# Gated linear attention and routed experts on one core: first rows stored later, banks returned later, a second alpha first, and early products of a second layer

## The chip, the core and the metric

The kernel runs on one core of a Trainium2 chip. The metric is the device time of one execution in microseconds (us). Five engines are named below: PE (TensorE, the matrix engine, with its weight loads PEld), DVE (VectorE), ACT (ScalarE), POOL (GpSimd) and SP (SyncE, which issues nearly all DMAs). Each engine works through its own instructions in the order in which the kernel emits them. PSUM has eight banks, which the kernel hands out as tiles.

## What is computed

The first half is a recurrent attention over 4 batches of 8 heads, 768 positions each, head size 48:

```python
for t in range(S):
    state = alpha[:, :, t, :, None] * state + einsum('bhd,bhde', k[:, :, t], v[:, :, t])
    y[:, :, t] = einsum('bhd,bhde->bhe', q[:, :, t], state)
```

The second half takes the 3072 rows of 384 numbers that come out and sends each to the one of eight experts with the largest logit of `x @ w_gate`. The expert computes `relu(x @ w1[e]) @ w2[e]` with 1024 hidden numbers, and the result is scaled by the softmax weight of that expert. Everything is float32.

## The kernel before

The 3072 rows are 24 chunks of 128 positions. A chunk `s` needs four loads (`load`, L300 to L309), one each of alpha, k, q and v. They are called a, k, q, v with the chunk's number below: a10 is alpha of chunk 10. Per chunk the kernel does this:

- `logs` (L328, ACT): logarithm of alpha. `cums` (L338): one PE product with a triangular mask gives cumulative sums in the single PSUM tile `cum`, from which ACT takes two exponentials, `icp` (L344) and `cpb` (L345). The next chunk's product can go into `cum` when `cpb` has been read out.
- `operands` (L360, mostly POOL): k times `icp` and q times `cpb`. `transposes` (L368): PE turns both, ACT and DVE copy them out as `kT` and `qT`.
- `scores` (L380), `reads`, `weighs`, `products`, `state`: the attention of the chunk and the state for the next. `rows` (L473) and `keep_rows` (L481) make the chunk's 128 output rows in the tile `xs`; `store_rows` (L489, SP) writes them to the DRAM tensor `x_rows`.

The order is written out by hand, under a manual schedule. Lines 631 to 700 start chunks 0 to 6. The loop of line 702 takes two chunks `s`, `s+1` in a pass, s = 2, 4, ..., 20. In a pass the calls for several chunks are mixed: `logs` and `cums` for s+5 and s+6, `operands` likewise, `transposes` for s+3 and s+4, `scores` for s+2 and s+3. SP's queue in a pass holds nine loads (`more_loads(2)`, `(2)`, `(5)` from the list `to_load`, L316), two small decay transfers and two stores of rows. Loads wait for nothing but a free buffer: a, k and q have five each, v has six; `xs` has three.

`keep_busy(n)` (L613) issues n products of a zero tile, whose result nobody reads. In the trace one float32 product is two matmul instructions.

After the loop the last two chunks are finished and the routing is worked out: `choose`, `slots_of`, `one_hots` on DVE, rank products and `tokens_of_slots` on PE (L589) into the tile `route`, then `slots(0)` (L605, DVE), which reads `route`, and the gathers of rows by POOL (L271). Each gathered block of 128 rows is turned by PE (`turn`, L966) and copied out by DVE into `xT`. The rows of expert 0's first 256 slots (`EB` = 2 blocks) are known earlier, so their first layer is emitted by a generator, `first_layer` (L787); `go_ahead(n)` takes its next n products, which serve as work for PE between the steps of the routing. It has 24 products (8 blocks `f` of the hidden layer by 3).

PSUM changes hands in this stretch: the pool `ps` (tiles `tp` with two banks, `sA`, `sB`, `xr`, `y0`, `y1`) is closed at L852, and `mps` (`hp` with three banks, `xtp` and `zp` with two each) takes the same seven banks.

The rest, from about 155 us on, is the eight experts in turn: `layer1` (L974), `layer2` (L987) and a scatter of finished rows by POOL (L1000), with the weights fetched ahead by SP.

Of the kernel before, what the change touches and what calls it, by code (L numbers as in the profile page):

```python
# [8 lines left out]
F32 = mybir.dt.float32  # L9
# [9 lines left out]
def kernel(  # L19
# [31 lines left out]
    C = 128  # L51
# [237 lines left out]
    with tc.tile_pool(name="ld", bufs=6) as ld, \  # L289
# [21 lines left out]
        def some_loads(names):  # L311
# [2 lines left out]


        to_load = [  # L316
            (n, x + d) for x in range(7, NT + 2)
            for n, d in (
                (("a", 1), ("k", 0), ("q", 0), ("v", -2)) if x == 7 else (("k", 0), ("v", -2), ("a", 1), ("q", 0))
            )  # L320
        ]


        def more_loads(n):
            for _ in range(min(n, len(to_load))):
# [42 lines left out]
        def transposes(s):  # L368
            d = st[s]
            for i, n in enumerate(("kT", "qT")):  # L370
                tp = ps.tile([C, NP, C], F32, name="tp", bufs=2)
                for p in range(NP):
                    nc.tensor.transpose(tp[:, p, :], pair(kqb[s % 4][:, i], p), ident[:])  # L373
                d[n] = work.tile([C, NP, C], F32, name=n, bufs=2 + i)
                if i:
                    nc.vector.tensor_copy(d[n][:], tp[:])  # L376
                else:
                    nc.scalar.copy(d[n][:], tp[:])
# [102 lines left out]

        def keep_rows(s):
            d = st[s]
            xs = work.tile([C, W], F32, name="xs", bufs=3)
            nc.scalar.copy(xs[:, :Dm].rearrange("t (p c) -> t p c", p=NP), d["xr"][:, :, :D2])  # L485
            nc.gpsimd.tensor_copy(xs[:, Dm:], lgn[:, s, :])
            d["xs"] = xs

        def store_rows(s):  # L489
            r0 = s * C + (s >= NT // 2)  # L490
            nc.sync.dma_start(x_d[r0 : r0 + C, :], st[s]["xs"][:])

        def choose(g):

# [133 lines left out]
        nc.scalar.preload_act_table_set("natural_log_exp_and_others")  # L628
        hots = []

        some_loads("a0 k0 q0 a1 k1 q1")
        first_consts()
        keep_busy(5)
        back_consts()
        for i in range(4):
            late_consts(i)
        logs(0)
        cums(0)
        keep_busy(3)
        operands(0, nc.vector, nc.vector)  # L640
        some_loads("a2 v0")
        decay_out(0, nc.scalar)
        logs(1)
        transposes(0)
        cums(1)
        operands(1)
        decay_in(0, nc.scalar)
        scores(0)
        keep_busy(3)
        some_loads("v1 k2 q2 a3 v2")  # L650
        logs(2)
        transposes(1)
# [48 lines left out]
        parts = fetch_parts(0)  # L701
        for s in range(2, NT - 2, 2):
            more_loads(2)
            if s == 2:
                store_rows(0)
            do(decay_out, s + 4)
            more_loads(2)

            for _ in range(8 if s > NT - 8 else 0):
                next(parts, None)  # L710
            y = results_of(s)
            reads(s)
            reads(s + 1)

            weighs(s, 0)
            weighs(s, 1)
            products(s + 1)
            products(s + 2)
            weighs(s + 1, 0)
            results_to(s, y, 0)  # L720
            weighs(s + 1, 1)
            results_to(s, y, 1)
            state(s + 1)
            do(logs, s + 5)
            if hots:
                one_hots(hots.pop(0))
            scores(s + 2)
            do(logs, s + 6)
            do(cums, s + 5)
            ranks = y[0][:].rearrange("r i p t -> r (i p t)")  # L730
            ranked = [rank_products(g, ranks[:, : len(g) * E]) for g in groups_of if g[-1] == s - 1]
            counts = ranks[:, C : C + E]
            if s in (TE, ORD):

                nc.tensor.matmul(
                    counts, lhsT=ones_sq[:], rhs=ohs[:, s, :], start=True, stop=True, skip_group_check=True,
                )
            if s == ORD:
                early_slots(ranks[:, 2 * C : 2 * C + EB * NQ])
                fetch_lot(0)  # L740
            for r in ranked if s < ORD else ():
                slots_of(*r)
            transposes(s + 3)
            do(operands, s + 5)
            state(s + 2)
            rows(s)
            keep_rows(s)
            store_rows(s - 1)
            if s == ORD:
                for r in ranked:  # L750
                    slots_of(*r)
                key = standing(counts[0:1, :])
                one_hots(hots.pop(0))
                one_hots(hots.pop(0))
                route = rps.tile([C, Dm], F32, name="cum")
                tokens_of_slots(0, TE)
            do(cums, s + 6)
            do(transposes, s + 4)
            more_loads(5)
            do(decay_in, s + 4)  # L760
            rows(s + 1)
            keep_rows(s + 1)
            if s == TE:
                close_early(counts[0:1, 0:1])

            chosen = [g for g in groups_of[:-2] if g[-1] == s + 1] + ([groups_of[-2]] if s == ORD else [])
            for g in chosen:
                choose(g)
            if hots and not chosen:
                one_hots(hots.pop(0))  # L770
            scores(s + 3)
            do(operands, s + 6)
            for g in chosen:
                sums(g)
            store_rows(s)
            if s == 2:

                nc.sync.dma_start(x_d[N // 2 : N // 2 + 1, :], zero_w[:])
            late_consts(s + 2)
            late_consts(s + 3)  # L780
            if hots and chosen:
                one_hots(hots.pop(0))
            for _ in range(4 if s == NT - 8 else 0):
                next(parts, None)
        for _ in parts:
            pass
        def first_layer():  # L787
            for f in range(FB):
                if f < 2:
                    hp = ps.tile([C, NP, C], F32, name="tp", bufs=2)[:].rearrange("r p t -> r (p t)")  # L790
                else:
                    hp = mps.tile([C, CAP], F32, name="hp", bufs=3)
                for a in range(DB):
                    nc.tensor.matmul(  # L794
                        hp[:, :EC], lhsT=w_t[0][0][:, a, f * C : (f + 1) * C], rhs=xT[0][:, a, :EC],
                        start=(a == 0), stop=(a == DB - 1),
                    )
                    if a < DB - 1:
                        yield
                nc.scalar.activation(h_t[0][:, f, :EC], hp[:, :EC], AF.Relu)  # L800
                yield

        ahead = first_layer()

        def go_ahead(n):
# [7 lines left out]
        y = results_of(s)  # L813
        reads(s)
        reads(s + 1)
        store_rows(s - 1)
        weighs(s, 0)
        weighs(s, 1)
        weighs(s + 1, 0)
# [8 lines left out]
            nc.scalar.copy(xT[0][:, :, k * C : (k + 1) * C], tp[:, :DB, :])  # L828
        rows(s)
        keep_rows(s)  # L830
        store_rows(s)
        go_ahead(3)
        for _ in range(3):
            one_hots(hots.pop(0))
        turns(key)
        rows(s + 1)
        keep_rows(s + 1)
        store_rows(s + 1)
        choose(groups_of[-1])
        sums(groups_of[-1])  # L840
        tokens_of_slots(TE, NT - 4)
# [3 lines left out]
        for i, (p, c, r) in enumerate((  # L845
# [3 lines left out]
        )):  # L849
            nc.tensor.matmul(p, lhsT=c[:], rhs=r, start=(i == 0), stop=(i == 2), skip_group_check=True)  # L850
        slots_of(groups_of[-1], pos)
        banks.close()  # L852
        mps = ctx.enter_context(tc.tile_pool(name="moe_ps", bufs=2, space=PSUM))
        go_ahead(4)
        one_hots(hots.pop(0))
        one_hots(hots.pop(0))
        tokens_of_slots(NT - 4, NT)
        nc.tensor.matmul(
            route[:, NC : NC + E], lhsT=ones_sq[:], rhs=ohs[:, NT, :], start=False, stop=True, skip_group_check=True,
        )  # L860
# [126 lines left out]
    def layer2(parts, gw, idx, apart):  # L987

        zp = mps.tile([C, Dm], F32, name="zp")
        wd = C if len(parts) == 1 else min(m for *_, m in parts)  # L990
        cuts = [(w2, h, c) for w2, h, c0, m in parts for c in range(c0, c0 + m, wd)]
        for f in range(FB):
            for i, (w2, h, c) in enumerate(cuts):
                nc.tensor.matmul(  # L994
                    zp[i * wd : (i + 1) * wd, :], lhsT=h[:, f, c : c + wd], rhs=w2[:, f, :],
                    start=(f == 0), stop=(f == FB - 1), skip_group_check=True,
                )
        zo = wk.tile([C, Dm], F32, name="zo", bufs=3)
        nc.scalar.activation(zo[:], zp[:], AF.Copy, scale=gw)  # L999
        ins = nc.gpsimd.indirect_dma_start(  # L1000
            out=out[:, :], out_offset=bass.IndirectOffsetOnAxis(ap=idx, axis=0),
            in_=zo[:], in_offset=None, bounds_check=N - 1, oob_is_err=False,
        )
        if apart:
            ins = getattr(ins, "ins", ins)
            tc.declare_no_dep(ins, group="rows_out", reason="disjoint rows")
            tc.add_to_no_dep_group("rows_out", ins)
# [20 lines left out]
        turn(*rows_t[k], *to)  # L1028

    def results(k):  # L1030
        parts = []
        for i in range(E):
            a, b = within(i, k)
# [14 lines left out]

    for i in range(E):
        if i == 0:  # L1050
            go_ahead(10)
            for k in range(EB, needed[0][-1] + 1):
                turn_block(k)
                go_ahead(3)
            go_ahead(99)
            layer1(w_t[0][0], xT[0], h_t[0], EC, cols[0])
        else:
            if i == E - 1:
# [84 lines left out]
```

## Time and profile before

| | us |
|---|---|
| median of three runs | 428.0 (427.19, 428.0, 1521.73) |
| the profiled execution, its own time | 427.69 |
| its span in the profile | 425.9 |
| PE busy | 418.0 |
| POOL / DVE / ACT busy | 141.0 / 138.3 / 108.0 |

The span is from the first to the last instruction of the profile; the time of the execution holds 1.8 us more around it. In the page's table of 40 slices each digit is the busy share, in tenths, of a stretch of about 10.6 us. The attention loop covers roughly 29 to 137 us, the routing 137 to 155 us, and the experts the rest.

### The profile page before, as it was taken

To read this page: it belongs to the slowest core of one execution; us is meant where nothing else is said; L and a number is where in the kernel's file an instruction comes from. 1 tells how busy PE (TensorE), PEld (TensorE's weight loads), DVE (VectorE), ACT (ScalarE), POOL (GpSimd) and SP (SyncE) were. 2 spreads that over 40 slices of the span, in tenths; PEclk is the share of its full clock that TensorE was granted. 3 is DMA by queue.
4 is the path that set the end of the run, shared out by engine and by line. 5 is a ranking of instruction groups with operands and counts; after the bars stand their busy time and mean duration, and the time that the engine had idled before them with its cause. 6 is when DMAs were issued, how large, how long until landed. Compare 5 with 4: busy or idle time off the path is not lost.

```text
span 425.9 us, 7698 instructions
## 1 busy us (share of the span) xinstructions
PE 418.0 (98%) x2990; PEld 283.5 (67%) x2990; DVE 138.3 (32%) x414; ACT 108.0 (25%) x230; POOL 141.0 (33%) x256
## 2 busy tenths in 40 slices
PE   8999999999999999999999999999999999999995
PEld 6888788888889887555554556655655455555452
DVE  6434567575768734712011101101201201111100
ACT  4565555555542221111111111011111110011011
POOL 5396677576675150250160120034010010011011
PEclk9999999999999999999999999999999999999999
DMA  8999998999976144994543600814720050000000
GB/s 172 181 174 209 187 204 186 204 206 212 186 212 208 56 115 143 393 372 152 179 133 94 234 32 0 304 45 112 246 94 12 5 181 20 0 33 20 1 33 30
DMA packets 132576, 59.43 MB, mean 140 GB/s; under 512 B 114614, under 2 KB 127452, under 8 KB 132538
## 3 DMA queue, kind: packets, MB, share of 16 engines
q1 hardware_dynamic: 127720, 48.96, 44.7%
q0 software_dynamic: 3328, 9.94, 7.1%
q8 instruction: 24, 0.39, 0.4%
q10 hardware_dynamic: 1490, 0.02, 0.2%
q14 instruction: 14, 0.11, 0.1%
HBM read 49.32 MB, written 9.98 MB: 139 GB/s over the span
## 4 chain that ended last, share of the span: by engine, by line
PE 61%; issue 28%; POOL 5%; SPq 2%; DMA 2%; ACT 1%; POOLq 0%; DVE 0%; ACTq 0%
PE zp L994 16%; PE hp L978 14%; PE sA L386 5%; PE y L430 5%; PE xr L478 4%; PE tp L373 4%; PE cum L341 3%; POOL out_dram L1000 3%; PE y L418 2%; PE hp L794 2%; PE xr L618 2%; PE xtp L970 1%; POOL xg L271 1%; PE sB L452 1%; DMA a_sb<-in_alpha_dram 1%
## 5 line engine op out<-in xcount | busy, mean ns | idle before, releaser
L994 PE MATMUL zp<-w,h_sb 128*128 128x384 f32 (+2 forms) x560 | 137.1, 487 | 0.0
L978 PE MATMUL hp<-xT,w 128*128 128x416 f32 (+5 forms) x384 | 123.9, 483 | 0.1
L994 PEld LDWEIGHTS zp<-w,h_sb 128*128 128x128 f32 (+2 forms) x560 | 73.6, 163 | 56.4 <-issue 14.8
L978 PEld LDWEIGHTS hp<-xT,w 128*128 128x128 f32 x384 | 71.6, 190 | 51.1 <-issue 31.0
L1000 POOL DMA_INDIRECT out_dram<-zo,o_idx x26 | 25.8, 991 | 213.5 <-ACT zo L999 208.5
L983 DVE TENSOR_SCALAR h_sb<-hp 128x416 f32<-128x416 f32 (+5 forms) x32 | 17.7, 554 | 148.1 <-PE hp L978 140.9
L999 ACT ACTIVATE zo<-zp,gw 128x384 f32<-128x384 f32 x26 | 15.1, 581 | 123.7 <-PE zp L994 114.5
L985 ACT ACTIVATE h_sb<-hp 128x416 f32<-128x416 f32 (+5 forms) x32 | 15.6, 487 | 106.5 <-PE hp L978 99.1
L271 POOL DMA_INDIRECT xg<-x_rows,g_idx x26 | 25.1, 966 | 11.1 <-issue 6.7
L386 PE MATMUL sA<-qT,kT 48*128 48x128 f32 x192 | 27.7, 284 | 0.2 <-DVE qT L376 0.2
L386 PE MATMUL sB<-qT,kT 48*128 48x128 f32 x192 | 27.7, 285 | 0.0
L972 DVE COPY xT<-xtp 128x384 f32<-128x384 f32 (+3 forms) x29 | 13.1, 485 | 44.6 <-PE xtp L970 43.2
L386 PEld LDWEIGHTS sA<-qT,kT 48*128 48x128 f32 x192 | 23.1, 187 | 4.7 <-issue 2.3
L364 POOL TENSOR_TENSOR kqb<-k_sb,icp 128x384 f32<-128x384 f32 x23 | 23.1, 1005 | 8.9 <-ACT icp L344 8.7
L430 PE MATMUL y<-dA,vb 128*64 128x128 f32 x192 | 25.9, 277 | 0.0
L373 PE MATMUL tp<-ident,kqb 128*128 128x128 f32 x192 | 25.4, 274 | 0.2 <-POOL kqb L366 0.2
L430 PE MATMUL y<-dB,vb 128*64 128x128 f32 x192 | 25.4, 277 | 0.0
L373 PEld LDWEIGHTS tp<-ident,kqb 128*128 128x128 f32 x192 | 21.8, 141 | 5.4 <-issue 2.7
L478 PE MATMUL xr<-back,yT 128*128 128x104 f32 x192 | 25.1, 274 | 0.0
L478 PEld LDWEIGHTS xr<-back,yT 128*128 128x128 f32 x192 | 23.6, 192 | 0.8 <-ACT xs L485 0.2
L376 DVE COPY qT<-tp 128x512 f32<-128x512 f32 x24 | 16.6, 690 | 21.0 <-PE tp L373 20.9
L386 PEld LDWEIGHTS sB<-qT,kT 48*128 48x128 f32 x192 | 23.1, 187 | 0.0
(179 smaller groups left out, 433.9 us busy)
## 6 DMA issues: line engine op xcount, KB each, us to landing
w<-in_moe_w_dram SPq DMA_DIRECT2D x14, 1536.0 KB
x_rows<-xs SPq DMA_DIRECT2D x24, 196.0 KB
a_sb<-in_alpha_dram SPq DMA_DIRECT2D x24, 192.0 KB
k_sb<-in_k_dram SPq DMA_DIRECT2D x24, 192.0 KB
q_sb<-in_q_dram SPq DMA_DIRECT2D x24, 192.0 KB
vb<-in_v_dram SPq DMA_DIRECT2D x24, 192.0 KB
w<-in_moe_w_dram SPq DMA_DIRECT2D x12, 128.0 KB
w<-in_moe_w_dram SPq DMA_DIRECT2D x8, 192.0 KB
```

What stands on the lines that cost most here:

```text
L271: nc.gpsimd.indirect_dma_start(out=xg[:, j, :], out_offset=None, in_=x_d[: N + 1 if n else TE * C + 1, :], in_offset=bass.IndirectOffsetOn ...
L364: k.tensor_tensor(kq[:, 0, :, :D], d["k"][:], heads(d["icp"]), op=ALU.mult)
L373: nc.tensor.transpose(tp[:, p, :], pair(kqb[s % 4][:, i], p), ident[:])
L376: nc.vector.tensor_copy(d[n][:], tp[:])
L386: nc.tensor.matmul(t[:, p, :], lhsT=d["kT"][r : r + D, p, :], rhs=d["qT"][r : r + D, p, :], start=True, stop=True,)
L430: nc.tensor.matmul(d["y"][h][at(p, a) : at(p, a) + DP, n, :], lhsT=d["v"][:, 2 * p + a, :], rhs=d["d" + "AB"[a]][:, p, :], start=(first an ...
L478: nc.tensor.matmul(xr[:, p, :], lhsT=d["yT"][:, p // (NP // 2), p % (NP // 2), :], rhs=back[:, p, :], start=True, stop=True)
L978: nc.tensor.matmul(hp[:, c0:c1], lhsT=w1[:, a, f * C : (f + 1) * C], rhs=xT[:, a, c0:c1], start=(a == 0), stop=(a == DB - 1),)
L983: nc.vector.tensor_relu(h[:, f, c0:c1], hp[:, c0:c1])
L985: nc.scalar.activation(h[:, f, c0:c1], hp[:, c0:c1], AF.Relu)
L994: nc.tensor.matmul(zp[i * wd : (i + 1) * wd, :], lhsT=h[:, f, c : c + wd], rhs=w2[:, f, :], start=(f == 0), stop=(f == FB - 1), skip_group ...
L1000: ins = nc.gpsimd.indirect_dma_start(out=out[:, :], out_offset=bass.IndirectOffsetOnAxis(ap=idx, axis=0), in_=zo[:], in_offset=None, bound ...
```

## The change

- `to_load` keeps its order, but for one place: alpha of chunk 10 is now loaded before v of chunk 7.
- The start loads a1 directly behind a0; it has one idle product fewer before chunk 0's cumulative sums (4 for 5), takes `logs(1)` straight behind `logs(0)`, puts `cums(1)` ahead of `transposes(0)`, and leaves out the three idle products after `scores(0)`. For chunk 0 alone, DVE copies `kT` and ACT copies `qT`; for the others it stays the other way.
- Rows are stored by a counter. The pass s=2 stores none (before: rows 0, 1 and 2), s=4 stores 0 and 1 (before: 3 and 4), s=6 stores 2, 3, 4 (before: 5 and 6), s=8 stores 5 to 8 (before: 7 and 8); from s=10 it is as before. `xs` has six buffers.
- `first_layer` uses `tp` for its first four blocks `f` instead of two, and goes on, after its 24 products, with the second layer of the two early blocks (16 products of 384 columns, into `zp`). `ps` is closed after `tokens_of_slots` and two more products of the generator. There are 12 products before the closing and 9 after it (before: 6 before and 14 after), then a turn, 3 products, a turn and 3 products again. The scaling and scatter of `layer2` become the function `write`, which `results` calls for the early blocks.

```diff
         to_load = [
-            (n, x + d) for x in range(7, NT + 2)
-            for n, d in (
-                (("a", 1), ("k", 0), ("q", 0), ("v", -2)) if x == 7 else (("k", 0), ("v", -2), ("a", 1), ("q", 0))
-            )
+            (n, x + {"a": 1, "v": -2}.get(n, 0)) for x in range(7, NT + 2)
+            for n in {7: "akqv", 9: "kavq"}.get(x, "kvaq")
         ]
...
-                if i:
+                if i == (s > 0):
                     nc.vector.tensor_copy(d[n][:], tp[:])
...
-            xs = work.tile([C, W], F32, name="xs", bufs=3)
+            xs = work.tile([C, W], F32, name="xs", bufs=6)
...
+        to_store = list(range(NT))
+
+        def stores(n):
+            for _ in range(n):
+                store_rows(to_store.pop(0))
...
-        some_loads("a0 k0 q0 a1 k1 q1")
+        some_loads("a0 a1 k0 q0 k1 q1")
         first_consts()
-        keep_busy(5)
+        keep_busy(4)
...
         logs(0)
+        logs(1)
         cums(0)
         keep_busy(3)
         operands(0, nc.vector, nc.vector)
         some_loads("a2 v0")
         decay_out(0, nc.scalar)
-        logs(1)
+        cums(1)
         transposes(0)
-        cums(1)
         operands(1)
         decay_in(0, nc.scalar)
         scores(0)
-        keep_busy(3)
...
-            if s == 2:
-                store_rows(0)
             do(decay_out, s + 4)
...
-            store_rows(s - 1)
+            stores({2: 0, 8: 2}.get(s, 1))
...
-            store_rows(s)
+            stores({2: 0, 6: 2, 8: 2}.get(s, 1))
...
         def first_layer():
             for f in range(FB):
-                if f < 2:
+                if f < 4:
...
+            for k in range(EB):
+                zps[k] = mps.tile([C, Dm], F32, name="zp")
+                for f in range(FB):
+                    nc.tensor.matmul(
+                        zps[k][:], lhsT=h_t[0][:, f, k * C : (k + 1) * C], rhs=w_t[0][1][:, f, :],
+                        start=(f == 0), stop=(f == FB - 1), skip_group_check=True,
+                    )
+                    if f == FB - 1:
+                        zdone.add(k)
+                    yield
...
         slots_of(groups_of[-1], pos)
-        banks.close()
-        mps = ctx.enter_context(tc.tile_pool(name="moe_ps", bufs=2, space=PSUM))
         go_ahead(4)
         one_hots(hots.pop(0))
         one_hots(hots.pop(0))
         tokens_of_slots(NT - 4, NT)
+        go_ahead(2)
+        banks.close()
+        mps = ctx.enter_context(tc.tile_pool(name="moe_ps", bufs=2, space=PSUM))
...
     def results(k):
+        if k < EB:
+            while k not in zdone:
+                next(ahead)
+            write(zps[k], gw[k], o_idx[:, k : k + 1], True)
+            return
...
-            go_ahead(10)
+            go_ahead(9)
             for k in range(EB, needed[0][-1] + 1):
                 turn_block(k)
                 go_ahead(3)
-            go_ahead(99)
```

More of the change, by code (lines that the diff above doesn't have):

```diff
@@ L801, in first_layer @@
                 yield
+            for k in range(EB):
[8 more added lines that the diff above has]
+                    yield
+        zps, zdone = {}, set()
         ahead = first_layer()
@@ L815 @@
         reads(s + 1)
-        store_rows(s - 1)
+        stores(1)
         weighs(s, 0)
@@ L830 @@
         keep_rows(s)
-        store_rows(s)
+        stores(1)
         go_ahead(3)
@@ L837 @@
         keep_rows(s + 1)
-        store_rows(s + 1)
+        stores(1)
         choose(groups_of[-1])
@@ L997, in layer2, with write @@
                 )
+        write(zp, gw, idx, apart)
+    def write(zp, gw, idx, apart):
         zo = wk.tile([C, Dm], F32, name="zo", bufs=3)
```

## The prediction

> **What bounds the kernel now.** I read the page first: the engines' busy time, then the slices.
>
> ```profile
> PE 418.0 (98%) x2990; PEld 283.5 (67%) x2990; DVE 138.3 (32%) x414; ACT 108.0 (25%) x230; POOL 141.0 (33%) x256
> ...
> PEclk9999999999999999999999999999999999999999
> DMA  8999998999976144994543600814720050000000
> ```
>
> PE is busy for 418.0 of 425.9 us at the full granted clock, so PE's own queue is the path, and only what PE waits for, or what it does in vain, can be saved. The DMA row says something else beside it: in the first ten slices, 0 to about 106 us, the 16 DMA engines are as full as PE. Next, the waits of PE:
>
> ```profile
> PE xr L618 <- DVE still L118: 1.3, 1, 1.3
> PE cum L341 <- ACT cpb L345: 0.6, 1, 0.6
> PE hp L794 <- ACT h_sb L800: 0.4, 1, 0.4
> ```
>
> Beyond the first, which is the launch, they come to little more than 1 us. The change touches the second and the third. Then PE's timeline of the start (start, duration, engine, line):
>
> ```profile
> 1.25 3.82 PE L618 MATMUL xr<-still 128*128 128x256 f32 x10 [1.25 <-DVE still L118]
> 5.00 0.88 PE L341 MATMUL cum<-ln,cmask 128*128 128x384 f32 x2
> 5.72 1.46 PE L618 MATMUL xr<-still 128*128 128x256 f32 x6
> 7.14 1.06 PE L373 MATMUL tp<-ident,kqb 128*128 128x128 f32 x8
> 8.05 0.81 PE L341 MATMUL cum<-ln,cmask 128*128 128x384 f32 x2
> ...
> 10.18 1.56 PE L618 MATMUL xr<-still 128*128 128x256 f32 x6
> 11.57 1.04 PE L373 MATMUL tp<-ident,kqb 128*128 128x128 f32 x8
> ```
>
> Busy is not useful here: L618 are idle products, and the six at 10.18 hold 1.39 us, start to next start. Third, the wait inside the loop, in ACT's and PE's timelines:
>
> ```profile
> 46.21 0.52 ACT L330 ACTIVATE ln<-a_sb 128x384 f32<-128x384 f32 x1 [1.29 <-DMA a_sb<-in_alpha_dram]
> ```
>
> ```profile
> 45.90 1.04 PE L478 MATMUL xr<-back,yT 128*128 128x104 f32 x8
> 47.55 0.91 PE L341 MATMUL cum<-ln,cmask 128*128 128x384 f32 x2 [0.61 <-ACT cpb L345]
> ```
>
> ACT stood 1.29 us for a10. Chunk 9's `icp` and `cpb` are queued behind that logarithm on ACT, and PE needs `cpb` read out before `cum` of chunk 10. The eight products of L478 take 0.87 us elsewhere in the loop, start to next start, and 1.65 us here (45.90 to 47.55). Cost: 0.77 us. Last, PE in the routing:
>
> ```profile
> 145.75 1.99 PE L794 MATMUL hp<-xT,w 128*128 128x256 f32 x8 [0.42 <-ACT h_sb L800]
> 147.58 0.40 PE L589 MATMUL cum<-oh_c,oh_r 128*128 128x128 f16 x4
> 147.81 0.17 PE L858 MATMUL cum<-ohs,ones_sq 128*128 128x8 f16 x1
> 147.84 4.56 PE L794 MATMUL hp<-xT,w 128*128 128x256 f32 x20
> 152.24 0.51 PE L970 MATMUL xtp<-ident,xg 128*128 128x128 f32 x3
> ```
>
> The first product in a returned bank waits for ACT's relu at L800, which reads another bank: the wait is for the last reader of the whole pool.
>
> **The start.** Taking out the six idle instructions alone would give next to nothing: chunk 1's transposes at 11.57 need POOL's second operand, which runs from 10.43 to 11.44. That in turn hangs on `icp` of chunk 1 (ACT, 8.89), hence on `cum` at 8.05 and `ln` of chunk 1 at 7.34. With a1 second its packets end where k0's ended, at 4.07 instead of 5.94 us in the trace's DMA packets. A load is seen by an engine about 0.85 us after its last packet (a10: packets to 45.28, landing 46.13 on the chain), so `ln` runs near 4.9. `cum` of chunk 1 then follows the idle products, at 7.1, once `cpb` of chunk 0 is read (6.30+0.48=6.78). `icp` goes from 8.89 to about 7.95, POOL's pair to 8.5 and 9.5, ending 10.5. Against it: `transposes(0)` is now behind that product, at 7.8 instead of 7.14, ends near 8.65, and ACT has `cpb` of chunk 1 (8.33 to 8.81) ahead of its `qT` copy (0.59). `scores(0)` starts near 9.5 instead of 9.08 and takes 1.09. So chunk 1's transposes start at 10.6, not 11.57: 0.97 us, I take 1.0. k0 and q0 come one load later (1.0 us each); q0 ends at 5.94, is seen at 6.8 and used at 6.92, just in time. The dropped fifth idle product (0.43 us) saves nothing, since `ln` of chunk 0 ends at 4.85 either way. Bounds: 0.1 (nothing but the 10.18 to 11.57 hole up to POOL's 11.44) and 1.4 (all idle products).
>
> The rest of the start to 28.65 runs from PE's side without much waiting, and its loads lie 2 to 5 us ahead of their use from a2 on (trace packets against first use; a6, the tightest, 1.8 us, of which 0.85 is landing). So 1.0 us carries to the loop if POOL and ACT follow, which they do in the same order.
>
> A clock risk: PE would now stand idle about 0.4 us at 4.5 and 0.8 us before `scores(0)`. In this trace the idle products step at 427 ns until about 4 us and at 216 ns after, and after the 0.61 us wait at 46.94 the steps are as before. I take nothing. [...]
>
> **Stores and loads.** Before a10 is issued (41.63), SP issued three stores, 0.76, 0.73 and 0.78 us of its queue; in the packets one costs 128 x 70.5 ns / 16 = 0.56 us of all DMA engines. All three go, and a10 also passes v7 (SP 0.43 us, a load's packets 1.0 us). So a10 comes at least 3 x 0.56 + 0.4 = 2.1 us sooner, and PE asks for it 1.0 us sooner: the 1.29 us wait of ACT is met by 2.1 - 1.0 = 1.1 plus the 0.5 us by which ACT may lag before PE feels it (1.29 against 0.77). The stall goes: 0.77 us. Bounds 0 and 0.77. Next late would be a12 (packets to 55.30, used 56.38, so 0.2 us ahead; PE feels it another 0.5 us later). Asked for 1.8 us sooner, it gains the same three stores, 1.7 us: just enough. v7, now one load later, is used a pass on: nothing.
>
> The catch-up puts one store more in s=6 and two more in s=8, 0.56 us of DMA each, 1.7 us. Cover: the loads that follow them are a16 (packets 74.65, use 78.10: 3.45) and a18 (84.51, 88.72: 4.21), less 0.85 landing and 1.8 earlier use: 0.8 and 1.5 us left. Nothing is paid; with that cover gone it would be up to 0.8 us. Two stores in a row block nothing on SP, as their rows are long made. Six `xs` buffers are refilled two passes after their store. Later passes gain room (a20 is 5.6 us ahead).
>
> **The routing.** The wait at 145.75 cost 145.75 - 145.20 = 0.55 us. Now four products run on in `tp` at once, 1.83 us, to 147.03. Then PE needs the last `one_hots` of DVE, which ended at 147.26 and is not moved: the tokens end at 147.4 instead of 147.81, a wait of 0.2 us. Two products (0.87) reach 148.27; L858 follows, 0.46 later than at 147.81, and `slots(0)` on DVE and the gathers behind it are late by as much. The first product after the closing waits for ACT's relu of block 3: as before 0.64 us from product's end to restart (145.11 to 145.75), thus 148.9. Nine products at 0.44 lead to the turn at 152.85, later than the gather: its packets ended at 151.80, so now 152.26, and PE could start 0.44 later. After the second turn three second-layer products (six at 0.322 us = 1.94) stand where PE waited 0.27 us for DVE's copy of `xT` (154.44 to 155.14 for one product of 0.43). Adding the pieces from 145.20: 9.71 us of the same work against 9.94. Gain 0.2 us. Bounds: -0.6 (the relu wait paid in full on top of a late gather) and +0.9 (no wait at all).
>
> The 16 products of the second layer are moved, not added (before: 5.16 us for a block at L994). The first turn for expert 1, and the weight fetches of SP behind its copy (164.6), move back by up to 1.7 us; expert 1 starts at 179.49, and a weight transfer of 1.5 MB at the 395 GB/s of that stretch takes 4 us. Nothing. DVE's index chain (167.3 to 175) moves likewise, and POOL's next gathers wait for the third `zo` at 180.5 anyway. From there to the end PE has no gap, so the gains arrive at the end undiminished.
>
> **Sum:** 1.0 + 0.77 + 0.2 = 1.97 us off the profiled execution's 427.69 (span 425.9 and 1.8 around it): 425.7. The median of the runs shown, 428.0, lies 0.3 above that execution and the fastest, 427.19, lies 0.5 below, so this is worth some 0.5%.
>
> **Rivals.**
> - *Loads set the pace.* The DMA engines are full to 106 us (0.89 to 1.02 by window), so PE, started earlier, waits at the next late load (a7, q7, a12). For: a12's 0.2 us. Against: three stores' 1.7 us. Then of 1.77 us only some 0.9 stays: 427.69 - 0.9 - 0.2 = 426.6.
> - *The stores do not free the loads*, because SP's queue is held by something else: the loads around 30 to 45 us take 0.4 to 1.8 us each to issue. Then the a10 wait stays, and grows by the earlier start: the start's gain is lost too, 427.5.
> - *The handover gets worse:* the relu wait plus a gather late by 0.46, -0.6 in place of +0.2: 426.5.
> - *The clock stays cold*, slower than before. Idle gaps at 4.5 and 8.7 us keep the 427 ns pace. Every us of PE work done at half pace costs one more; it turns the sum when this lasts for more than 1.97 us of work beyond 4 us. To `scores(0)` that is `cum` 0.72, idle products 1.43, `cum` 0.75, transposes 0.87: 3.8 us more, 429.5. For: only the slow first 2.7 us. Against: the steps after other short waits.
> - *More is won:* with POOL's 0.44 us hold of the transposes at 25.5 to 26.8 gone and 0.7 of the routing's 0.8 us of waits left above: 427.69 - 3.1 = 424.6.
>
> **How the numbers follow.** The forecast 425.7 gets 0.60 (its own range 425.0 to 426.3), loads 0.16, stores 0.06, handover 0.08, cold clock 0.04, more 0.06. The range 424.4 to 427.4 holds all but the cold clock, the stores' case and some of the spread between runs (0.8 us here). A difference of under 2%, 8.6 us, is about what a measurement of this kernel can tell from no change; no case reaches it, so within 2% gets 0.97, slower 0.02 for a wait that I don't see, faster 0.01.
>
> **What would show it.** Chunk 1's transposes near 10.6 us and the loop's first `reads` (28.65) near 27.6; no wait of L341 near 46 us, with ACT's `ln` of a10 not waiting for DMA; a wait of L589 near 147.3 minus the shift and one of L794 for ACT's relu after L858; L978's first product without a wait. Wrong would make it: L618-like pace after 4 us, new waits of ACT for `a_sb` between 50 and 90 us, or a wait of L970 for the gather.

## The result and the profile after

| | before | after |
|---|---|---|
| median of four executions each, us | 428.26 | 426.66 |
| the profiled execution, own time (span), us | 427.69 (425.9) | 427.45 (425.7) |
| PE busy in it, us | 418.0 | 417.5 |

Three of the executions reported here were far slower than all others and are left out of the ratios: one of the kernel before here (1521.73 us; without it its median is 428.0), one of `pool_later` (616.85) and one of the kernel before beside `best5` (484.34).

The ratio is 0.9974, with a 95% interval of 0.995 to 0.9999: some 1.1 us off 428, where 1.97 was forecast. The time is inside the range and the sign is right, but a good part of the gain is missing. The profiled execution shows still less, 0.24 us. Both gaps need explaining.

From the page of the changed kernel, the busy time of PE:

```profile
PE 417.5 (98%) x2982; PEld 282.6 (66%) x2982; DVE 139.8 (33%) x414; ACT 107.8 (25%) x230; POOL 141.1 (33%) x256
```

Eight idle instructions are gone (2990 to 2982), but not their 2 us. PE's waits (line numbers are up by 3 around the start, down by 3 in the attention):

```profile
PE xr L621 <- DVE still L118: 1.3, 1, 1.3
PE sA L383 <- ACT qT L375: 0.7, 1, 0.7
PE tp L370 <- DVE qT L373: 0.6, 1, 0.6
PE hp L795 <- ACT h_sb L801: 0.5, 1, 0.5
```

The wait of `cum` for `cpb` is gone, as forecast. A wait of the transposes (`tp`) for DVE's copy `qT` has come in its place, of the same 0.6 us. PE's timeline of the start:

```profile
1.25 3.78 PE L621 MATMUL xr<-still 128*128 128x256 f32 x8 [1.25 <-DVE still L118]
5.00 1.62 PE L338 MATMUL cum<-ln,cmask 128*128 128x384 f32 x2
6.41 1.83 PE L621 MATMUL xr<-still 128*128 128x256 f32 x6
8.08 0.81 PE L338 MATMUL cum<-ln,cmask 128*128 128x384 f32 x2
8.72 1.04 PE L370 MATMUL tp<-ident,kqb 128*128 128x128 f32 x8
10.44 0.37 PE L383 MATMUL sA<-qT,kT 48*128 48x128 f32 x1 [0.67 <-ACT qT L375]
...
11.53 1.09 PE L370 MATMUL tp<-ident,kqb 128*128 128x128 f32 x8
```

The new order is there, with the 0.7 us wait that the working had. Yet chunk 1's transposes start at 11.53, against 11.57 before: nothing is won. The same two instructions of `cum` at 5.00 last 1.41 us to the next start (6.41), where they took 0.72 before: PE still ran at half pace. The trace's clock records put full pace at 7.16 us here and at 4.11 in the profile of before.

The pass s=4, first on ACT, then PE, DVE and POOL:

```profile
44.84 0.53 ACT L327 ACTIVATE ln<-a_sb 128x384 f32<-128x384 f32 x1
```

```profile
45.92 1.04 PE L475 MATMUL xr<-back,yT 128*128 128x104 f32 x8
46.80 0.83 PE L338 MATMUL cum<-ln,cmask 128*128 128x384 f32 x2
47.47 0.60 PE L370 MATMUL tp<-ident,kqb 128*128 128x128 f32 x4
48.63 0.66 PE L370 MATMUL tp<-ident,kqb 128*128 128x128 f32 x4 [0.56 <-DVE qT L373]
49.24 1.14 PE L475 MATMUL xr<-back,yT 128*128 128x104 f32 x8
```

```profile
45.43 0.19 DVE L524 TENSOR_REDUCE slot_i<-own 128x4 int32<-128x32 f32 x1
45.65 0.40 DVE L526 TENSOR_SCALAR rc_i<-slot_i 128x4 int32<-128x4 int32 x1
45.97 1.05 DVE L527 TENSOR_SCALAR rc_i<-slot_i 128x4 int32<-128x4 int32 x1
47.05 0.93 DVE L531 CAST rc<-rc_i 128x8 f32<-128x8 int32 x1
47.90 0.68 DVE L373 COPY qT<-tp 128x512 f32<-128x512 f32 x1
```

```profile
45.40 0.62 POOL L390 TENSOR_SCALAR_AFFINE_SELECT dB<-dB 128x512 f32<-128x512 f32 x1
46.00 0.99 POOL L361 TENSOR_TENSOR kqb<-k_sb,icp 128x384 f32<-128x384 f32 x1
46.95 0.99 POOL L363 TENSOR_TENSOR kqb<-q_sb,cpb 128x384 f32<-128x384 f32 x1
```

ACT's logarithm of a10 waits for nothing: the packets of a10 end at 41.98, in before at 45.28. `cum` follows L475 after 0.88 us, its usual step. But then the eight transposes take 1.77 us from start to next start (47.47 to 49.24), where the loop's median is 0.91. They need a `tp` bank that DVE's copy `qT` has yet to read. This copy is 1.7 us late (47.90; before 46.21), because three tiny DVE instructions, of 4 to 8 numbers per partition, took 0.40, 1.05 and 0.93 us. In the trace of before the first took 0.39 as well, but the last two 0.16 and 0.17; DVE and POOL there:

```profile
45.94 0.16 DVE L524 TENSOR_SCALAR rc_i<-slot_i 128x4 int32<-128x4 int32 x1
46.13 0.17 DVE L528 CAST rc<-rc_i 128x8 f32<-128x8 int32 x1
```

```profile
47.20 1.00 POOL L364 TENSOR_TENSOR kqb<-k_sb,icp 128x384 f32<-128x384 f32 x1 [1.20 <-ACT icp L344]
```

In the changed kernel each of the three ends when a POOL instruction ends: 46.05 and 46.02, 47.02 and 46.99, 47.98 and 47.95. In before, POOL stood idle at that time: its pair waited for `icp` until 47.20, since ACT waited for a10. The late load had kept POOL out of DVE's way. From the first product of `reads` in the pass s=4 to that of the next pass, the kernel before takes 11.53 us and the changed one 11.68: the stall is gone, and the pass is no shorter.

The routing:

```profile
145.41 1.97 PE L795 MATMUL tp<-xT,w 128*128 128x256 f32 x8
147.22 0.53 PE L592 MATMUL cum<-oh_c,oh_r 128*128 128x128 f16 x4
147.59 1.08 PE L795 MATMUL tp<-xT,w 128*128 128x256 f32 x4
148.51 0.17 PE L872 MATMUL cum<-ohs,ones_sq 128*128 128x8 f16 x1
149.14 4.15 PE L795 MATMUL hp<-xT,w 128*128 128x256 f32 x18 [0.47 <-ACT h_sb L801]
...
155.09 2.10 PE L807 MATMUL zp<-w,h_sb 128*128 128x384 f32 x6
157.02 1.30 PE L992 MATMUL hp<-xT,w 128*128 128x192 f32 x7
```

This went as reckoned. The relu's wait is 0.63 us from L872 to the next start (forecast 0.64), there is none for the gather, and none before L992. From the products at L863 (L850 before) to the experts it is 155.14 - 145.11 = 10.03 us before, and 157.02 - 145.34 = 11.68 now, of which 1.93 are moved second-layer products: 0.28 shorter (forecast 0.2).

### The profile page after: what moved, and what is told of

It reads as the page before. It is cut to its first block, busy times and chain, and to the rows that moved or that the text cites. A ratio compares the mean times of both kernels' runs of the same rounds, so it can differ in the third digit from the quotient of the medians.

```text
span 425.7 us, 7674 instructions
## 1 busy us (share of the span) xinstructions
PE 417.5 (98%) x2982; PEld 282.6 (66%) x2982; DVE 139.8 (33%) x414; ACT 107.8 (25%) x230; POOL 141.1 (33%) x256
## 4 chain that ended last, share of the span: by engine, by line
PE 65%; issue 28%; POOL 4%; DVE 1%; ACT 1%; POOLq 0%
PE hp L992 14%; PE zp L1008 13%; PE sA L383 6%; PE y L427 5%; PE xr L475 5%; PE tp L370 4%; PE cum L338 4%; POOL out_dram L1017 3%; PE y L415 3%; PE zp L807 2%; PE sB L449 1%; PE hp L795 1%; PE tp L795 1%; PE xr L621 1%; PE xtp L984 1%
## 5 line engine op out<-in xcount | busy, mean ns | idle before, releaser
L1008 PE MATMUL zp<-w,h_sb 128*128 128x384 f32 (+2 forms) x528 | 126.6, 487 | 0.0
L992 PE MATMUL hp<-xT,w 128*128 128x416 f32 (+5 forms) x384 | 123.9, 482 | 0.0
L992 PEld LDWEIGHTS hp<-xT,w 128*128 128x128 f32 x384 | 71.7, 190 | 50.9 <-issue 30.5
L1008 PEld LDWEIGHTS zp<-w,h_sb 128*128 128x128 f32 (+2 forms) x528 | 67.6, 161 | 52.7 <-issue 14.8
L475 PE MATMUL xr<-back,yT 128*128 128x104 f32 x192 | 25.2, 274 | 0.0
L475 PEld LDWEIGHTS xr<-back,yT 128*128 128x128 f32 x192 | 23.6, 192 | 1.0 <-ACT xs L482 0.3
L390 POOL TENSOR_SCALAR_AFFINE_SELECT dB<-dB 128x512 f32<-128x512 f32 x24 | 15.5, 648 | 24.0 <-ACT dB L389 20.4
```

The lines of the kernel that those rows point to most:

```text
L475: nc.tensor.matmul(xr[:, p, :], lhsT=d["yT"][:, p // (NP // 2), p % (NP // 2), :], rhs=back[:, p, :], start=True, stop=True)
L992: nc.tensor.matmul(hp[:, c0:c1], lhsT=w1[:, a, f * C : (f + 1) * C], rhs=xT[:, a, c0:c1], start=(a == 0), stop=(a == DB - 1),)
L1008: nc.tensor.matmul(zp[i * wd : (i + 1) * wd, :], lhsT=h[:, f, c : c + wd], rhs=w2[:, f, :], start=(f == 0), stop=(f == FB - 1), skip_group ...
```

## The experiments

The theory was that the start's gain is real but was hidden by the clock of one execution, and that the a10 stall was exchanged for the DVE wait. The first rival was that a part of the change does not do its work at all; the second that loads are the pace. Kernels that are named together ran on one chip; times are medians of 11 or 12 executions unless something else is said. The diffs are excerpts.

**Each part alone, and the change again.** `after_again` is the changed kernel. Each of the others is the kernel before with one part of the diff: `start_only` the order of the start, `stores_only` the later stores, the load list and six `xs`, `handover_only` the generator, the closing and `write`.

```diff
# start_only
-        some_loads("a0 k0 q0 a1 k1 q1")
+        some_loads("a0 a1 k0 q0 k1 q1")
...
+        logs(1)
         cums(0)
...
+        cums(1)
         transposes(0)
-        cums(1)
# stores_only
-            store_rows(s - 1)
+            stores({2: 0, 8: 2}.get(s, 1))
# handover_only
-        banks.close()
...
         tokens_of_slots(NT - 4, NT)
+        go_ahead(2)
+        banks.close()
```

> The changed kernel unaltered, for a second profile. Theory 1 (the start's gain of 1.0 us is there, but only in an execution whose TensorE clock is full by about 5 us; in the profiled one it was full from 7.25 us, against 4.11 us in the kernel before): this profile shows chunk 1's transposes near 10.6 us if its clock is full by 5 us and near 11.5 us if by 7 us, and the span follows, 424.7 or 425.7. Theory 2 (the fewer idle products themselves delay the clock, whatever the run): the clock is full from about 7.2 us again and the transposes stand near 11.5 us. Both: the wait for qT of L373 near 48 us, 0.5 to 0.9 us. Timed against the kernel before: -1.2 us by theory 1 where most runs are warm, -0.3 us by theory 2.

> The kernel before with the start of the change alone (a1 second, fewer idle products, logs and cums of chunk 1 earlier, kT by DVE and qT by ACT for chunk 0). Theory 1 (loads pace the passes s=2 and s=4): PE arrives up to 1.0 us sooner at the pass s=4 and waits that much longer for alpha of chunk 10, in all 0 to -0.3 us. Theory 2 (the start's gain carries through): -1.0 us.

> The kernel before with the deferred stores, six xs buffers and alpha of chunk 10 ahead of v of chunk 7 alone. Theory 1 (the wait for alpha of chunk 10 goes, and POOL's two operand instructions, which it had held back, then run over DVE's slot arithmetic, so that DVE's qT copy and PE's transposes come late): within 0.2 us of the kernel before, with a wait of 0.5 to 0.9 us of PE's transposes for qT near 48 us. Theory 2 (the stall goes as predicted): -0.8 us, no wait there.

> The kernel before with the later return of the banks and the second layer's products between the turns alone. Theory 1 (as in the profile of the changed kernel): -0.3 us, one wait of 0.6 us for ACT's relu after the routing's last product, none before layer1. Theory 2 (nothing but a moved wait): 0.

| run | median, us (before: 428.04) | ratio, 95% interval |
|---|---|---|
| after_again | 426.72 | 0.997 (0.9958 to 0.9982) |
| start_only | 427.60 | 1.0002 (0.9987 to 1.0017) |
| stores_only | 428.24 | 1.0012 (1.0003 to 1.0021) |
| handover_only | 427.65 | 0.9995 (0.9985 to 1.0006) |

The whole is won again, and no part alone wins it. In `start_only` chunk 1's transposes start at 10.79 and the loop at 27.93, but PE still waits for `cpb` in the pass s=4:

```profile
45.18 1.04 PE L478 MATMUL xr<-back,yT 128*128 128x104 f32 x8
46.60 0.91 PE L341 MATMUL cum<-ln,cmask 128*128 128x384 f32 x2 [0.38 <-ACT cpb L345]
```

The eight products of L478 take 1.42 us, 0.55 more than usual, and ACT's gap for a10 is 1.06 us. The profile of `stores_only` has no such wait, but has the `tp` wait of 0.6 us, and its DVE instructions take 1.05 and 0.93 us. So this wait comes with the earlier a10, not with the new start. That `start_only`'s own profile (426.65) is nearly 1 us better than its median is not explained by this; what its other executions waited for stays open.

**Pairs, and two cures for the DVE wait.** `start_stores` and `start_hand` put two parts together. `slots_later` and `pool_later` are the changed kernel with DVE's slot work, or POOL's pair, moved in the pass s=4 alone.

```diff
# slots_later
-            for r in ranked if s < ORD else ():
+            for r in ranked if 4 < s < ORD else ():
                 slots_of(*r)
             transposes(s + 3)
+            for r in ranked if s == 4 else ():
+                slots_of(*r)
# pool_later
-            do(operands, s + 5)
+            if s != 4:
+                do(operands, s + 5)
             state(s + 2)
             rows(s)
             keep_rows(s)
+            if s == 4:
+                do(operands, s + 5)
```

> The changed kernel with one move: in the pass s=4 DVE's slot arithmetic (slots_of) is emitted behind transposes(s+3), so behind DVE's qT copy. Theory 1 (DVE's integer operations wait for POOL's operand instructions, and the qT copy behind them is what PE waits for): the wait of PE near 48 us is gone, 0.7 us less than the changed kernel, about -2.0 us against the kernel before; the integer operations still take about 1 us each if they meet POOL's. Theory 2 (PE waits there for something else, a load or POOL's operands): no change against the changed kernel, -1.3 us.

> The changed kernel with one move on POOL: in the pass s=4 operands(s+5) is emitted behind keep_rows(s), so that POOL stands idle while DVE does its slot arithmetic. DVE's order is as in the changed kernel. Theory 1 (the two engines block each other): DVE's operations at L526, L527, L531 of that pass take 0.2 us each instead of 0.4, 1.05 and 0.93; the wait of PE for qT is gone, about -2.0 us against the kernel before. Theory 2 (DVE's operations are slow there by themselves): they stay at about 1 us and nothing is gained.

> The start and the stores of the change, without the handover. Theory 1 (each alone is eaten: the start by the wait for alpha of chunk 10, the stores by the wait for qT; together the start's gain is kept): -1.0 us against the kernel before, though each alone measured within 0.5 us of it. Theory 2 (the parts add up as measured alone): +0.5 us.

> The start and the handover of the change, without the deferred stores. Theory 1 (without the deferral the wait for alpha of chunk 10 holds the pass s=4): -0.3 to -0.8 us against the kernel before, ACT waits for that load, and DVE's slot arithmetic is quick. Theory 2 (the deferral is of no use for the start's gain): -1.3 us, as the whole change.

| run | median, us (before: 428.04) | ratio, 95% interval |
|---|---|---|
| slots_later | 427.39 | 0.9983 (0.9972 to 0.9995) |
| pool_later (6 executions) | 426.48 | 0.9957 (0.994 to 0.9974) |
| start_stores | 426.94 | 0.9973 (0.9961 to 0.9986) |
| start_hand | 427.57 | 0.999 (0.9975 to 1.0006) |

By the ratios, start and stores together give what the whole gives, and the start without the stores gives little. Why the stores help it is not seen in the profiles: `start_hand` still waits 0.8 us for `cpb`, but its pass s=4 takes 11.7 us, and so does that of `start_stores`, with the DVE wait in place of this one. In `slots_later` the copy `qT` is in time, but the wait only moves. DVE's timeline, and PE's waits:

```profile
46.10 1.29 DVE L526 TENSOR_SCALAR rc_i<-slot_i 128x4 int32<-128x4 int32 x1
47.31 0.16 DVE L527 TENSOR_SCALAR rc_i<-slot_i 128x4 int32<-128x4 int32 x1
...
47.58 0.18 DVE L477 TENSOR_REDUCE lgn<-xr 128x8 f32<-128x32 f32 x1
```

```profile
PE xr L475 <- ACT xs L482: 0.9, 1, 0.9
```

The first slot instruction now ends only with POOL's L466 (46.10 + 1.29 = 47.39; L466 ends at 47.37), and `lgn` behind it, which reads `xr`, is late; PE, which wants `xr` back, pays 0.9 us. In `pool_later`, where POOL's pair runs at 47.10 to 49.08, DVE loses 0.4 us at most and PE's pass has no wait:

```profile
45.10 0.41 DVE L526 TENSOR_SCALAR rc_i<-slot_i 128x4 int32<-128x4 int32 x1
45.42 0.56 DVE L527 TENSOR_SCALAR rc_i<-slot_i 128x4 int32<-128x4 int32 x1
46.02 0.17 DVE L531 CAST rc<-rc_i 128x8 f32<-128x8 int32 x1
46.10 0.68 DVE L373 COPY qT<-tp 128x512 f32<-128x512 f32 x1
```

The pass takes 10.67 us from `reads` to `reads` (39.17 to 49.84), against 11.68 in the changed kernel: moving POOL's two instructions, and nothing else, gives back 1.0 us there. That shows the cause of the wait. In the ratios this gain does not stand out: the interval of `pool_later` overlaps those of the changed kernel (0.997 above, 0.998 below). In its profile something else is late instead; PE's and POOL's timelines:

```profile
94.54 0.67 PE L415 MATMUL y<-qT,Ub 48*64 48x128 f32 x16 [0.94 <-POOL Ub L466]
```

```profile
90.33 0.51 POOL L466 TENSOR_TENSOR Ub<-accA,Eb 128x192 f32<-128x192 f32 x1 [3.46 <-DMA Eb<-decay_rows]
```

POOL stood 3.46 us for the small decay load `Eb`, and its queue was late by that: the rival that loads set the pace, but with a load that the prediction had not looked at.

**The kernel before again, five idle products, and the decay load.** `before_look1` and `before_look2` are the kernel before, one execution each. `kb5` is the changed kernel with five idle products at the start, `pool_decay` is `pool_later` with the decay load ahead of five big loads on SP.

```diff
# kb5
-        keep_busy(4)
+        keep_busy(5)
# pool_decay, beside the lines of pool_later
-            more_loads(5)
             do(decay_in, s + 4)
+            more_loads(5)
```

> The kernel before, unaltered, for another profile of its start. Theory 1 (the moment at which the clock becomes full is a matter of chance in either kernel, within about 3 us; at the same moment the new start is 1.2 to 1.4 us ahead): the full clock comes anywhere between 4 and 7.3 us, and chunk 1's transposes start at 11.5 us for 4.1 and later by 0.4 us for each us that the clock is late. Theory 2 (the kernel before, with its fifth idle product, always gets the full clock by 6 us): 4 to 6 us again.

> As the run before it: a second look at the kernel before. Theory 1: the full clock between 4 and 7.3 us and the transposes of chunk 1 later by 0.4 us for each us. Theory 2: by 6 us.

> The changed kernel with five idle products in place of four ahead of chunk 0's cumulative sums. Theory 1 (chance): within 0.3 us of the changed kernel, -1.1 to -1.3 us against the kernel before, and up to 0.2 us worse where the clock is late, as the fifth product then ends after 5 us. Theory 2 (the dropped product delays the clock): full clock by 6 us, and 0.5 us or more better than the changed kernel.

> pool_later with the small load of the decay (decay_in, SP) ahead of the five loads of its pass instead of behind them, in all passes. Theory 1 (with PE 1.8 us ahead the decay load is the next late thing: POOL's U waited up to 3.9 us for it, and PE 1.2 us in one pass of pool_later's profile): no wait of L415 for POOL's U, -2.0 us against the kernel before and a narrower spread. Theory 2 (that wait was a single event): as pool_later, -1.7 us, or worse if SP then waits for the decay to land in DRAM.

The two took 427.69 and 427.18 us, with full pace from 6.00 and 5.17 us and chunk 1's transposes at 12.35 and 11.94. So the 4.11 of the first profile was an early case. The a10 stall varies too. PE's pass s=4 in the second:

```profile
46.27 1.04 PE L478 MATMUL xr<-back,yT 128*128 128x104 f32 x8
47.14 0.83 PE L341 MATMUL cum<-ln,cmask 128*128 128x384 f32 x2
```

L478 takes 0.87 us there, with no wait of PE at all, though ACT stood 0.39 us for a10; the pass takes 10.67 us from `reads` to `reads`. In the first it takes 10.99, in `handover_only`, which has the old loads, 10.97, and in the profile that the prediction was made from 11.53: 0.32, 0.30 and 0.86 more.

`kb5` measured 427.41 against 427.77, ratio 0.9993 (0.9979 to 1.0008). This is no better than four products, though its profile has full pace at 4.20, chunk 1 at 10.46 and no DVE wait. The order of the pass s=4 is that of the changed kernel, but a10 was late once more: ACT stood 0.41 us for it, POOL's pair began at 45.26, and DVE was done with the slot work by then:

```profile
44.90 0.16 DVE L527 TENSOR_SCALAR rc_i<-slot_i 128x4 int32<-128x4 int32 x1
45.09 0.17 DVE L531 CAST rc<-rc_i 128x8 f32<-128x8 int32 x1
```

The pass takes 10.68 us. What the kernel wins so far it loses at L415 to the decay load (two waits, 1.0 us together). `pool_decay` measured 426.50, ratio 0.9967 (0.9954 to 0.998), and its profile has no wait at L415 any more.

**The number of idle products.** I took it then that each idle product less delays the full pace. Two executions each, on one chip (before beside them: 427.64), with five products (`kb5_look1`, `kb5_look2`) and with two (`kb2_look1`, `kb2_look2`):

```diff
-        keep_busy(4)
+        keep_busy(2)
```

> The changed kernel with five idle products, for the moment of the full clock. Theory 1 (chance): from 4 to 7.3 us. Theory 2 (activity counts): 4 to 6 us.

> As kb5_look1, a second look. Theory 1: from 4 to 7.3 us. Theory 2: 4 to 6 us.

> The changed kernel with two idle products in place of four ahead of chunk 0's sums: PE is idle from about 3 to 5 us. Theory 1 (chance): full clock anywhere from 4 to 7.3 us. Theory 2 (the activity before 5 us counts): later than 7 us, as the activity up to 3 us is lost to it, and chunk 1's transposes 0.4 us later for each us.

> As kb2_look1, a second look. Theory 1: full clock from 4 to 7.3 us. Theory 2: later than 7 us.

With five: 425.51 and 426.27 us. With two: 428.01 and 428.25, the whole gain gone. The pass s=4 goes the way it went in `kb5`: `kb5_look1`, where ACT stood 0.29 us for a10, takes 10.68 us; `kb5_look2`, where it did not wait, takes 11.13, with 1.05 us for L527. The start of `kb2_look1` on PE:

```profile
1.25 2.08 PE L621 MATMUL xr<-still 128*128 128x256 f32 x4 [1.25 <-DVE still L118]
4.99 1.62 PE L338 MATMUL cum<-ln,cmask 128*128 128x384 f32 x2 [1.67 <-ACT ln L327]
```

Full pace comes at 8.13 (8.65 in the other), and chunk 1 at 12.01 (12.26).

**The best of it, against the changed kernel.** `best5` is `pool_decay` with five idle products, `after_side` the changed kernel beside it on the same chip (before: 427.93).

```diff
# best5, beside the lines of pool_decay
-        keep_busy(4)
+        keep_busy(5)
```

> The changed kernel with five idle products ahead of chunk 0's sums, operands(s+5) of the pass s=4 behind keep_rows(s) on POOL, and decay_in ahead of the five loads of each pass. If these three causes are all: full clock by 6 us, chunk 1's transposes at 10.5 to 11.0, no PE wait in the passes s=2 to s=20 over 0.3 us, 2.2 to 2.8 us less than the kernel before and 1 us less than the changed kernel. Rival (another load is next late): no better than pool_decay, -1.4 us.

> The changed kernel, unaltered, beside best5 on the same chip: -1.1 to -1.3 us against the kernel before, full clock between 4.6 and 7.2 us.

`best5` took 426.29 (5 executions), ratio 0.9954 (0.9941 to 0.9967); `after_side` 426.99, ratio 0.998 (0.997 to 0.9991). So there is a version 0.7 us better than the change, on this chip, 2.0 us off the kernel before by the ratio where 2.2 to 2.8 were expected. It changes three things at once, and this run does not tell what each is worth. Its waits of PE behind the launch:

```profile
PE sA L383 <- ACT qT L375: 0.7, 1, 0.7
PE hp L798 <- ACT h_sb L804: 0.5, 1, 0.5
PE tp L370 <- POOL kqb L363: 0.2, 1, 0.2
```

No wait of the loop above 0.2 is left. But full pace came at 7.44 in this profile, with five products: the theory of the count falls between four and five.

**The clock, over all profiles.** What fits all twenty is a grid. The time from the rise to half pace's return at the end is 419.83 or 419.84 us in nine of them and 416.42 or 416.43 in the other eleven, one step of 3.41 us apart, with nothing between. So I took the share of the last 3.41 us in which PE had matmuls running, at each rise and one step ahead of it:

| profile | idle products | rise, us | chunk 1's transposes, us | PE's share to the rise | one step earlier |
|---|---|---|---|---|---|
| before | 5 | 4.11 | 11.57 | 0.84 | 0.00 |
| kb5 | 5 | 4.20 | 10.46 | 0.86 | 0.00 |
| slots_later | 4 | 4.61 | 10.46 | 0.98 | 0.00 |
| before_look2 | 5 | 5.17 | 11.94 | 1.00 | 0.15 |
| start_only | 4 | 5.67 | 10.79 | 1.00 | 0.29 |
| before_look1 | 5 | 6.00 | 12.35 | 1.00 | 0.39 |
| pool_later | 4 | 6.05 | 10.98 | 1.00 | 0.41 |
| after_again | 4 | 6.62 | 11.26 | 1.00 | 0.57 |
| after | 4 | 7.16 | 11.53 | 1.00 | 0.73 |
| best5 | 5 | 7.44 | 11.95 | 1.00 | 0.81 |
| kb2_look1 | 2 | 8.13 | 12.01 | 0.92 | 0.59 |
| kb2_look2 | 2 | 8.65 | 12.26 | 1.00 | 0.51 |

Every rise is the first step with a share of at least 0.84, and no step with 0.81 or less opened the clock; the eight profiles left out here fit too. Where the grid lies against the start I take to be chance. The rise falls between 4.1 and 7.4 us with five idle products and between 4.6 and 7.2 with four, and with two it comes at 8.13 and 8.65, after a step that their gap from 3.3 to 5.0 leaves at a share of 0.59 and 0.51. That it is chance is not shown: the nine profiles with five products rise at 5.2 us in the mean and the nine with four at 6.4, which the shares do not account for. The 0.7 us gap ahead of `scores(0)` (0.67 in the changed kernel) made the clock fall in none of the profiles that have it.

## Why the prediction was right and wrong, step by step

- **The start, 1.0 us:** the mechanism was right and the size a little small. At like clocks the new start is ahead by 11.57 - 10.46 = 1.1 us (rises at 4.11 and 4.20) and by 12.35 - 10.98 = 1.4 us (6.00 and 6.05). What was wrong was to take the profiled execution's start as the kernel's: its rise was the earliest of all twenty, that of the changed kernel's profile among the latest, and each us of later rise costs some 0.4 us (12.35 against 11.57 in the kernel before for rises at 6.00 and 4.11; 11.53 against 10.46 with four products for 7.16 and 4.61). These two profiles hid the term. Over all profiles, whatever their clocks, the loop's first `reads` come at 28.32 us in the mean of the nine with the new start and four products, and at 29.04 in the five with the old start: 0.7 us.
- **"The stall goes: 0.77 us. Bounds 0 and 0.77":** this is the step that failed, in two ways. The stall did go, with the load 3.3 us earlier. But it was worth 0.86, 0.32, 0.30 and 0 us of the pass s=4 in four profiles with the old loads and the old start, some 0.4 in the mean; the upper bound, read from one profile, was taken as the value. And what came next was not a12, which costs PE nothing, but POOL, released 1.2 us earlier on top of DVE's slot work. The working asked only for the next load and put what POOL would then do at nothing, without a reason. The pass takes 11.68 us in the changed kernel's profile, 1.0 more than without any wait. The net, 0.4 won and 1.0 lost, is a loss of some 0.6 us, below the lower bound of 0. `stores_only`, the part by itself, measured that: 1.0012, so +0.5 us (0.1 to 0.9; +0.2 by the medians). A load 0.3 to 0.4 us late was better than one in time: where ACT stood that long for a10, in `before_look2`, `kb5` and `kb5_look1`, the pass took 10.67 to 10.68, no longer than with POOL's pair moved.
- **The handover, 0.2 us:** right, 0.28 in the profile, and 0.9995 (-0.2 us) for the part alone, with an interval that holds 1.
- **The catch-up of stores:** right, each pass from s=6 on takes what it took, within 0.12 us.
- **The sum:** -1.1 to -1.4, +0.5 and -0.3 make -0.9 to -1.2, which meets 0.9974 (-1.1), and the other two measurements of the change, 0.997 (-1.3) and 0.998 (-0.9). This takes the start at like clocks; with the 0.7 us of all profiles it would be -0.5. The parts measured alone add up to +0.4 by the ratios and to -0.6 by the medians, so how much of the whole is interplay stays open. That the time still fell inside the forecast's range is in part luck: one term was too small, another had the wrong sign. The profiles of before caught early clocks (4.11 to 6.00) and those of the changed kernel late ones (6.62 to 7.16), which is why they show less than the medians. That the other executions have their clocks by the same chance is inferred; they left no trace.
- **The rivals:** *stores do not free the loads* and *the handover gets worse* did not come. *The clock stays cold* came in no profile with four or five products by way of a gap; what varies is the phase. *Loads set the pace* came where PE ran earlier still: not at a7, q7 or a12 but at the small `Eb`, in `pool_later` and `kb5`. The exchange of the stall for a DVE wait was in none of the rivals.
- **What stays open:** why the clock rose later with four products than with five; why the stores help the start, as the ratios say; why `kb5`'s median is 0.9 us above `pool_decay`'s and `start_only`'s 1 us above its profile. The decay load and the a10 wait are seen in their profiles, but not in how many executions they occur.

## What to carry to other kernels

When a stall goes, list every engine that it held back, not only the next load: each starts earlier, and what it then runs beside may be worse than the stall. A term of less than 1 us is not read from one execution; a second profile of the unchanged kernel would have shown both the clock's phase and the stall's spread. Compare starts only at the same clock.

## What the runs showed of the hardware

- Three small DVE instructions on SBUF tiles (L526, L527, L531) ended with POOL's instructions: in the changed kernel they took 0.40, 1.05 and 0.93 us, each ending 0.03 us after one of POOL's, and in `slots_later` the first took 1.29 while POOL ran two `TENSOR_TENSOR`s in a row. In the kernel before, where POOL stood idle, the last two took 0.16 and 0.17 us; in `pool_later`, with POOL's pair moved, 0.56 and 0.17. Not every DVE instruction was longer: `lgn`, read from PSUM, took 0.18 us ahead of POOL's pair in `pool_later` and 0.19 beside it, and the reduce L524 0.19 beside POOL's L390 in the changed kernel. Why the three are held up, no run shows.
- The clock rose only on the 3.41 us grid, at PE shares of 0.84 and more, and at none of 0.81 or less (the ends of products as the profile models them). The windows view shows a granted clock of 1.00 from the start all the same (0 to 4 us, in the profiles of before and after alike), and the prediction's PEclk row a 9, so half pace is seen only in the trace's clock records and in the steps: 427 ns for an idle product's instruction, 216 after the rise.
